# Strided attention in products of three residues, in 64 by 64 tiles of TensorE, and another order of the first batch's attention

## The chip, the cores and the metric

The kernel runs on one core of one Trainium2 chip. The metric is device time in microseconds, from the start of the program on the core to its end. Durations of single instructions come from one profiled execution.

## The reference

For 4 batches, 8 heads, 576 positions and 64 numbers a head, masked attention is computed; the first four heads look at the last 32 positions, the other four only at positions with the same remainder by 32. Two feed-forward nets follow on the 2304 rows.

```python
stride = 32
scores = scale * np.matmul(q, k.transpose(0, 1, 3, 2))
rel = pos[:, None] - pos[None, :]
mask_local = (rel >= 0) & (rel < stride)
mask_strided = (rel >= 0) & (pos[None, :] % stride == pos[:, None] % stride)
...
scores = scores - np.max(scores, axis=-1, keepdims=True)
attn = np.exp(scores)
attn = attn / (np.sum(attn, axis=-1, keepdims=True) + 1e-09)
return np.matmul(attn, v).astype(np.float32)
...
h = np.maximum(np.maximum(x @ w1, x @ w2), x @ w3)      # 512 to 768, then @ w_out to 512
g = np.maximum(h, 0.0) + alpha * np.minimum(h, 0.0)     # h = x @ w_in, 512 to 2048; then @ w_out
```

## The kernel before

The host sorts the positions of the strided heads by remainder (residue): 32 residues of 18 positions each, so that a strided head's scores are 32 blocks of 18 by 18 on the diagonal. Heads go in pairs, `cc` = 0, 1 for the local heads and 2, 3 for the strided ones; head `j` of a pair lies on 64 partitions.

`attention_tasks` handles half a pair, a unit `(b, cc, hf)`. A strided unit takes groups of six residues (108 positions, three groups) or seven (126, two groups), from the table `RG`: one product of 108 by 108 or 126 by 126 per head and group into a bank of PSUM (scores, line 353), a mask and the minimum of the negated scores on VectorE (line 361; `mask_s` for strided heads, `mask_l` and `mask_l0` for local ones), exponential and sum on ScalarE (line 368, with `accum_out`, so that each is followed by a read of the accumulator), reciprocals of the sums (lines 379, 380), normalising (on VectorE, line 397 or 394, or ScalarE, line 392), transposes on TensorE (line 408), a copy to SBUF (line 269), and the product with the values (line 437). The result is split in a high and a low part, `x`, by `part_tasks` (cast and subtraction, lines 269 and 272). Local units do the same with products of 32 by 64 (line 346), and `local_values` (line 483) does two units at once.

The nets use each number as a high and a low part: three products in place of one. A gate unit (`gate_products`, line 682) is 12 products of 288 columns with one weight tile `w`, and needs `x` of all four pairs of its half (order of the pairs: 2, 3, 0, 1). The weights arrive as 64-bit floating point numbers, and `from_double` and `split_tasks` turn them into 32-bit words and parts on ScalarE (lines 534, 543, 269) and VectorE (lines 538, 547, 550, 272). Each of the 18 gate weights of a batch's first layer is a word of this kind; they stay for the later batches.

Attention of all batches, the words and the first net of batches 0 to 2 are tasks of a planner, `Weave`: each has costs by engine, a position, needs and buffers, and the planner gives out one order, which every engine's queue then keeps. Attention of batch 0 has positions ahead of all gates, that of batches 1 to 3 lies between the gates of the batch before. SP issues all loads in one queue, in the planner's order too; a load that waits for its buffer holds those behind it. `UNREAD` puts products on a constant tile `warm_r` ahead of some tasks of TensorE (fillers, line 218); nobody reads their result. `build_constants` makes the masks and the identity on GpSimd ahead of all tasks.

Of the kernel before, what the change touches and what calls it, by code (L numbers as in the profile page):

```python
# [32 lines left out]
RG = [(0, 6), (6, 6), (12, 6), (18, 7), (25, 7)]  # L33
# [7 lines left out]
UNREAD = {(0, 3, 0): 6, ((0, 2, 0), 0): 8, ((0, 3, 0), 1): 7, ((0, 1, 0), 0): 9}  # L41
# [7 lines left out]
COST = (500, 1000)  # L49


class Weave:
# [11 lines left out]
    def __init__(self, rings):  # L64
        self.rings, self.made = dict(rings), {ring: [] for ring in rings}
        self.tasks, self.givers, self.users, self.banks, self.stores = [], {}, {}, set(), set()
        self.order = {ring: [] for ring in ("q", "v", "e", "pt", "x", "word")}
# [100 lines left out]
def attention_maxout_prelu_kernel(  # L168
# [19 lines left out]
    warm_r = const.tile([P, P], F32R, name="warm_r")  # L188
    mask_l = const.tile([QT, KW], F32, name="mask_l")
    mask_l0 = const.tile([QT, KW], F32, name="mask_l0")  # L190
    mask_s = const.tile([P, 126], F32, name="mask_s")
    alpha_sb = const.tile([P, NF2], F32, name="alpha_sb")

    def build_constants():
        g = nc.gpsimd
        nc.vector.memset(warm_r.bitcast(F32), 1.0)
        unread(bank(), WARM)
        make_identity(nc, ident)
        g.memset(mask_s, 0.0)
        ms = mask_s.rearrange("p (r a) -> p r a", a=NA)  # L200
        g.affine_select(out=ms, in_=ms, compare_op=ALU.is_ge, fill=BIG, base=0,
                        pattern=[[-NA, 7], [-1, NA]], channel_multiplier=1)
        g.affine_select(out=ms, in_=ms, compare_op=ALU.is_ge, fill=BIG, base=NA - 1,
                        pattern=[[NA, 7], [0, NA]], channel_multiplier=-1)
# [8 lines left out]
        g.memset(mask_l0[:STRIDE, :STRIDE], BIG)  # L213

# [38 lines left out]
    smp = pool(ax, "smp", 4)  # L253
    raw_p = pool(conv_x, "raw", 3, "right")
    words_p = pool(conv_x, "words", 6, "right")
    front_x = ExitStack()
    front_qk = pool(front_x, "fqk", 1, "right")
    ps = psx.enter_context(tc.tile_pool(name="ps", bufs=8, space=PSUM))
# [5 lines left out]
    weave = Weave({"bank": 8, "q": 2, "third q": 1, "v": 3, "e": 3, "pt": 4, "x": 11, "t": 4, "h": 12,  # L264
# [19 lines left out]
    def geometry(cc, hf):  # L284

        if cc < 2:
            return QT, KW, [(QT * t, QT * t, t, mask_l0 if t == 0 else mask_l)
                            for t in range(3 * hf, 3 * hf + 3)]
        gs = range(0, 3) if hf == 0 else range(3, 5)
        n = RG[gs[0]][1] * NA  # L290
        return n, n, [(RG[g][0] * NA, RG[g][0] * NA, g, mask_s) for g in gs]

    xt = {}

    def load_task(b, cc, pos):
        qk, vk = ("q", b, cc), ("v", b, cc)
# [1155 lines left out]
```

## Time and profile before

| | |
|---|---|
| time, median of 3 runs | 738.41 us (736.92 to 738.92) |
| the profiled execution's own time | 737.37 us |
| its span, first to last instruction | 735.5 us |
| granted TensorE clock | 1.00 |
| TensorE busy | 727.1 us, 99% |
| VectorE busy | 623.0 us, 85% |
| ScalarE busy | 459.1 us, 62% |
| GpSimd busy | 29.2 us, 4% |

The rows further below are read so: PE is TensorE, PEld its weight loads, DVE VectorE, ACT ScalarE, POOL GpSimd, SP the engine that issues transfers. A timeline's row gives the start, the time from the first start to the last end, the engine, the line of the kernel, the operation, output<-input, shape and count; behind it in brackets the idle time ahead of it and what ended it. Ends of products are modelled and overlap the next start, so the cost of a group is best taken from its start to the next group's start. A product of 32-bit numbers stands there twice.

### The profile page before, as it was taken

How to read it: one execution, taken by the hardware profiler on the slowest of the kernel's cores; microseconds unless marked ns; L12 is line 12 of the kernel's file. 1: busy time of each engine (PE TensorE's matmuls, PEld its weight loads, DVE VectorE, ACT ScalarE, POOL GpSimd, SP SyncE). 2: the span in 40 equal slices, each digit the busy share in tenths (PEclk: the TensorE clock that was granted, in tenths of full speed). 3: DMA queues.
4: the chain of work that ended last, by engine and by line, in shares of the span. 5: the costliest groups of instructions: out<-in, count | busy, mean ns of one | idle time of the engine just before them, and what ended most of it. 6: DMA issues, size and time to landing. Idle time of an engine off the chain costs nothing.

```text
span 735.5 us, 17464 instructions
## 1 busy us (share of the span) xinstructions
PE 727.1 (99%) x6306; PEld 706.1 (96%) x6306; DVE 623.0 (85%) x1680; ACT 459.1 (62%) x1221; POOL 29.2 (4%) x49
## 2 busy tenths in 40 slices
PE   8899999999999999999999999999999999999998
PEld 6799999999999999999999999999999999999997
DVE  5898897899898899669779988979989888888896
ACT  7997987688596676342365665625566644656561
POOL 2000000000000000055100000000000000000000
PEclk9999999999999999999999999999999999999999
DMA  8776689996998767788999799999689999867362
GB/s 294 224 262 207 220 289 343 340 326 230 361 320 298 266 231 249 244 336 317 358 326 350 252 322 327 403 381 388 238 305 308 368 401 365 296 233 253 113 206 68
DMA packets 90086, 213.63 MB, mean 290 GB/s; under 512 B 11152, under 2 KB 41360, under 8 KB 90000
## 3 DMA queue, kind: packets, MB, share of 16 engines
q1 hardware_dynamic: 90000, 212.51, 82.1%
q8 instruction: 50, 0.82, 0.4%
q14 instruction: 36, 0.29, 0.1%
HBM read 156.38 MB, written 56.10 MB: 289 GB/s over the span
## 4 chain that ended last, share of the span: by engine, by line
PE 96%; DVE 2%; ACT 1%; POOL 1%; issue 0%; POOLq 0%
PE bank L682 26%; PE ph L1289 24%; PE po L1090 15%; PE bank L704 11%; PE bank L855 5%; PE po L1096 4%; PE ph L1090 4%; PE po L1100 2%; PE bank L408 2%; PE bank L483 1%; PE bank L437 1%; PE bank L346 1%; PE bank L353 1%; ACT e L368 1%; DVE e L361 1%; PE bank L218 1%
## 5 line engine op out<-in xcount | busy, mean ns | idle before, releaser
L1289 PE MATMUL ph<-x,w 128*128 128x384 f32 x990 | 200.0, 337 | 0.0
L682 PE MATMUL bank<-x,w 128*128 128x288 f32 x1440 | 198.5, 296 | 0.0
L682 PEld LDWEIGHTS bank<-x,w 128*128 128x128 f32 x1440 | 191.9, 188 | 1.6 <-issue 0.2
L1289 PEld LDWEIGHTS ph<-x,w 128*128 128x128 f32 x990 | 166.3, 188 | 0.8
L1090 PE MATMUL po<-w,g 128*128 128x256 f32 x936 | 135.6, 281 | 0.0
L1090 PEld LDWEIGHTS po<-w,g 128*128 128x128 f32 x936 | 130.1, 189 | 0.4
L1295 DVE TENSOR_TENSOR c<-ph,c 128x384 f32<-128x384 f32 x165 | 89.5, 555 | 31.1 <-PE ph L1289 30.3
L1083 ACT CAST g<-c 128x384 fp32r<-128x384 f32 x93 | 47.2, 507 | 90.9 <-DVE c L1273 51.7
L704 PE MATMUL bank<-h,w 128*128 128x288 f32 x576 | 79.7, 297 | 0.0
L704 PEld LDWEIGHTS bank<-h,w 128*128 128x128 f32 x576 | 76.8, 188 | 0.6
L272 DVE TENSOR_TENSOR w<-word,w 128x512 fp32r<-128x512 f32 x100 | 63.2, 642 | 13.2 <-ACT w L269 12.6
L1233 ACT ACTIVATE c<-c 128x384 f32<-128x384 f32 x96 | 50.6, 528 | 33.4 <-DVE c L1295 32.3
L368 ACT ACTIVATE e<-e,nm 96x64 f32<-96x64 f32 (+2 forms) x176 | 63.5, 372 | 5.5 <-DVE nm L361 5.2
L269 ACT CAST w<-word 128x512 fp32r<-128x512 f32 x100 | 57.4, 592 | 14.7 <-DMA wh<-w 7.3
L1234 ACT ACTIVATE c<-c,nalpha 128x384 f32<-128x384 f32 x96 | 59.4, 619 | 3.1
L1238 DVE SCALAR_TENSOR_TENSOR c<-c 128x384 f32<-128x384 f32 x96 | 53.1, 553 | 5.9 <-ACT c L1234 5.9
L1084 DVE TENSOR_TENSOR g<-c,g 128x384 fp32r<-128x384 f32 x96 | 53.0, 552 | 0.9 <-ACT g L1083 0.5
L772 DVE TENSOR_TENSOR t<-bank,t 128x288 f32<-128x288 f32 x72 | 32.7, 454 | 12.8 <-PE bank L682 8.9
L1084 DVE TENSOR_TENSOR g<-k,g 128x384 fp32r<-128x384 f32 x72 | 37.1, 556 | 7.5 <-ACT g L1083 7.5
L1096 PE MATMUL po<-w,g 128*128 128x512 f32 x120 | 43.0, 398 | 0.0
L534 ACT ACTIVATE word<-raw 128x512 f32<-128x512 f32 x56 | 37.2, 683 | 8.5 <-DMA raw<-in_w 4.8
L1273 DVE TENSOR_TENSOR k<-c 128x384 f32<-128x384 f32 x72 | 37.9, 551 | 0.0
(114 smaller groups left out, 918.8 us busy)
## 6 DMA issues: line engine op xcount, KB each, us to landing
w<-wh SPq DMA_DIRECT2D x72, 512.0 KB, 5.4
raw<-in_w SPq DMA_DIRECT2D x50, 512.0 KB, 5.3
w<-wo SPq DMA_DIRECT2D x48, 512.0 KB, 5.9
w<-wp SPq DMA_DIRECT2D x36, 512.0 KB, 6.4
wh<-w SPq DMA_DIRECT2D x24, 512.0 KB, 4.4
xd<-xst SPq DMA_DIRECT2D x28, 384.0 KB, 3.2
x<-xd SPq DMA_DIRECT2D x28, 384.0 KB, 8.2
ws<-w SPq DMA_DIRECT2D x12, 512.0 KB, 4.2
```

The source lines that it names most:

```text
L269: (nc.scalar.copy if e == "ACT" else nc.vector.tensor_copy)(out_, in_)
L272: nc.vector.tensor_tensor(out=out_, in0=x, in1=y, op=ALU.subtract)
L368: nc.scalar.activation(tl[ek][:nq, j, i, :nk], tl[ek][:nq, j, i, :nk], AF.Exp, bias=tl["nm", u][:nq, j, i:i + 1], scale=-1.0, accum_out=tl ...
L682: nc.tensor.matmul(acc, words["gate", f, g][:, wi, cc * P:(cc + 1) * P], xt[b, cc, hf][:, xi, :], start=n == 0, stop=n == 3 * NCC - 1)
L704: nc.tensor.matmul(acc, words["mix", f][:, wi, dc * P:(dc + 1) * P], st["h", hf, f][:, xi, :], start=n == 0, stop=n == 3 * NF1 - 1)
L1084: return g, lambda: nc.vector.tensor_tensor(out=g[:, 1], in0=x, in1=g[:, 0].bitcast(F32), op=ALU.subtract)
L1090: nc.tensor.matmul(bank[:, NH * half:NH * (half + 1)], g[:, gi, t * P:(t + 1) * P], w[:, wi, off:off + NH], start=first and i == 0, stop=l ...
L1096: nc.tensor.matmul(bank.rearrange("p (s n) -> p s n", n=NH), g[:, 0, t * P:(t + 1) * P], w[:, :, off:off + NH], start=first, stop=last)
L1234: nc.scalar.activation(a, a, AF.Copy, scale=nalpha[:, f:f + 1])
L1238: nc.vector.scalar_tensor_tensor(out=a, in0=h, scalar=0.0, in1=a, op0=ALU.max, op1=ALU.add)
L1289: nc.tensor.matmul(bank, words["h", n, i][:, wi, off + c * P:off + (c + 1) * P], x2h[blk, k, c][:, xi, :], start=m == 0, stop=m == 5)
L1295: nc.vector.tensor_tensor(out=out_, in0=bank, in1=other, op=ALU.add)
```

## The change

Strided units are now whole pairs, `(b, cc)`, in a function of their own, `strided_tasks`. The residues are taken in threes (54 positions, 11 groups, the last of two residues; the twelfth place repeats the eleventh). A group's scores are a product of 64 by 54 per head, whose output lies on partitions 0 to 63 for even groups and 64 to 127 for odd ones, so that four products use four 64 by 64 tiles of TensorE. The exponentials lie 64 apart in one of two fixed tiles, whose gaps are zeroed once, and two groups are transposed at a time (128 by 128). The values are products of 64 by 54 in the same four tiles. `q`, `k` and `v` of strided pairs are padded on the host (608 and 768 columns in place of 576 and 640).

In the first batch the loads of all four pairs' q and k come ahead of the values', the two strided pairs and the first half of the local ones come ahead of the gates, and the second half of the local ones later, among them. Four units of this batch (`REDUCED`) have no `accum_out` in their exponentials: VectorE sums them in one reduction for each unit. GpSimd makes `mask_s` first, and the other masks and the identity in `build_more`, given out behind the first masking task. Fillers stand in other places, and the buffers of `x`, local scores and some others differ by one.

The core of the diff:

```diff
-RG = [(0, 6), (6, 6), (12, 6), (18, 7), (25, 7)]
+NR = 3
+RW = NR * NA
+NG2 = 11
+SP = S + STRIDE
-UNREAD = {(0, 3, 0): 6, ((0, 2, 0), 0): 8, ((0, 3, 0), 1): 7, ((0, 1, 0), 0): 9}
+UNREAD = {(0, 3): 2, (0, 0, 0): 2, (0, 1, 0): 3, ((0, 2), "t", 0): 4, ((0, 2), "s"): 2, ((0, 3), "s"): 3, (0, 0, 0, 0): 6}
+AFTER = {(1, 2): [("begun", 0, ("t", 0, 0, 0))]}
+REDUCED = {(0, 2), (0, 3), (0, 0, 0), (0, 1, 0)}
...
-    xp = pool(x0x, "xp", 11)
+    xp = pool(x0x, "xp", 10)
-    ep = pool(ax, "ep", 3)
+    ep = pool(ax, "ep", 2)
+    e_strided = [esp.tile([P, 2, 6, D], F32, tag=f"es{i}", name="es") for i in range(2)]
...
+    def strided_tasks(b, cc, pos, step):
+        u = (b, cc)
...
+            for g in range(12):
+                at = RW * min(g, NG2 - 1)
+                t = 2 * (g % 6 // 2) + g // 6
+                for j in range(2):
+                    rows = slice(D * j, D * (j + 1))
+                    nc.tensor.matmul(sc[j][D * (g % 2):D * (g % 2 + 1), RW * t:RW * (t + 1)],
+                                     q[rows, at:at + D], k[rows, at:at + RW], start=True, stop=True)
...
+            def masked(_, i=i):
+                for t in (2 * i, 2 * i + 1):
+                    for j in heads:
+                        nc.vector.tensor_tensor_reduce(
+                            out=tl[ek][:, j, t, :RW], in0=tl["sc", u][j][:, RW * t:RW * (t + 1)], in1=mask_s,
+                            scale=-SCALE, scalar=3.0e38, op0=ALU.add, op1=ALU.min,
+                            accum_out=tl["mx", u][:, j, t:t + 1])
+                if (u, i) == ((0, 2), 0):
+                    build_more()
...
+                        sums = {} if u in REDUCED else dict(accum_out=tl["ss", u][:, j, t:t + 1])
+                        nc.scalar.activation(e, e, AF.Exp, bias=tl["mx", u][:, j, t:t + 1], scale=-1.0, **sums)
...
+        def normalise(_):
+            e, ss, sr = tl[ek][:, :, :, :RW], tl["ss", u], tl["sr", u]
+            if u in REDUCED:
+                nc.vector.tensor_reduce(out=ss, in_=e, op=ALU.add, axis=mybir.AxisListType.X)
+            nc.vector.tensor_scalar_add(sr, ss, 1e-9)
+            nc.vector.reciprocal(sr, sr)
+            nc.vector.tensor_tensor(out=e, in0=e, in1=sr.unsqueeze(3).to_broadcast([P, 2, 6, RW]),
+                                    op=ALU.mult)
...
+                for i in range(3):
+                    nc.tensor.transpose(tr[:, P * i:P * (i + 1)],
+                                        tl[ek][:, j, 2 * i:2 * i + 2].rearrange("p t k -> p (t k)"), ident)
...
+            for g in range(6):
+                for t in range(2):
+                    n = RW if 6 * t + g < NG2 - 1 else 2 * NA
+                    if 6 * t + g < NG2:
+                        rows = slice(D * t, D * t + RW)
+                        for j in heads:
+                            nc.tensor.matmul(tl[pvs[t]][D * j:D * (j + 1), RW * g:RW * g + n], v[rows, j, g],
+                                             tl[pts[j]][rows, D * g:D * g + n], start=True, stop=True)
...
+        if b == 0:
+            when = {2: -60, 3: -56, (0, 0): -50, (1, 0): -48, ("l", 0): -43.2,
+                    (0, 1): -4, (1, 1): -2, ("l", 1): 2.8}
+            loads = {("q", 2): -80, ("q", 3): -79, ("q", 0): -78, ("q", 1): -76, ("v", 2): -54, ("v", 3): -52,
+                     ("v", 0, 0): -44, ("v", 1, 0): -44 + 0.5, ("v", 0, 1): -6, ("v", 1, 1): -6 + 0.5}
+            attention(b, when, loads, 2.4)
+            continue
```

What stands where on the engines. First TensorE at the end of the first batch's attention, before; L346 are local scores, L353 strided scores, L408 transposes, L483 local values, L218 fillers, and L682 gate products.

```order
L346 MATMUL bank<-k,q 32x64 x18
L218 MATMUL bank<-warm_r 128x512 x9
L408 MATMUL bank<-ident,e 128x96 x3
L353 MATMUL bank<-k,q 108x108 x6
L483 MATMUL bank<-pt,v 64x32 x36
L408 MATMUL bank<-ident,e 128x96 x3
L353 MATMUL bank<-k,q 126x126 x4
L682 MATMUL bank<-x,w 128x288 x12
L408 MATMUL bank<-ident,e 128x96 x3
L682 MATMUL bank<-x,w 128x288 x12
L483 MATMUL bank<-pt,v 64x32 x36
L682 MATMUL bank<-x,w 128x288 x216
```

The same place after, from the transposes of the first half on; here L397 are local transposes, L352 local scores, L426 local values, L228 fillers, L740 gate products, and L465 strided scores of batch 1.

```order
L397 MATMUL bank<-ident,e 128x96 x3
L352 MATMUL bank<-k,q 32x64 x18
L397 MATMUL bank<-ident,e 128x96 x3
L352 MATMUL bank<-k,q 32x64 x18
L426 MATMUL bank<-pt,v 64x32 x36
L228 MATMUL bank<-warm_r 128x512 x6
L740 MATMUL bank<-x,w 128x288 x36
L397 MATMUL bank<-ident,e 128x96 x6
L740 MATMUL bank<-x,w 128x288 x12
L426 MATMUL bank<-pt,v 64x32 x36
L465 MATMUL bank<-k,q 64x54 x24
L740 MATMUL bank<-x,w 128x288 x192
```

Three gate units now stand ahead of the second half's transposes, and four ahead of its values, where two stood behind nearly all of the batch's attention.

ScalarE at its beginning, before: L368 are exponentials with their sums, L269 copies of transposed scores (`pt`) and casts of `x`, L534 the first step of a word.

```order
L368 ACTIVATE e,sm<-e,nm 108x108 x6
L368 ACTIVATE e,sm<-e,nm 126x126 x4
L368 ACTIVATE e,sm<-e,nm 108x108 x4
L269 COPY pt<-bank 108x324 x2
L368 ACTIVATE e,sm<-e,nm 108x108 x2
L269 COPY pt<-bank 126x252 x2
L368 ACTIVATE e,sm<-e,nm 126x126 x2
L269 CAST x<-bank 128x9x18 x2
L368 ACTIVATE e,sm<-e,nm 126x126 x2
L269 CAST x<-bank 128x9x14 x2
L368 ACTIVATE e,sm<-e,nm 96x64 x6
L534 ACTIVATE word<-raw 128x512 x2
```

The same after: L487 are strided exponentials and L368 local ones, both without sums here, L283 copies and casts, L590 and L599 steps of words.

```order
L487 ACTIVATE es<-es,mx 128x54 x24
L368 ACTIVATE e<-e,nm 96x64 x8
L283 COPY pt<-bank 128x384 x2
L368 ACTIVATE e<-e,nm 96x64 x4
L590 ACTIVATE word<-raw 128x512
L283 CAST x<-bank 128x9x18
L283 CAST x<-bank 128x9x14
L283 CAST x<-bank 128x9x18
L283 CAST x<-bank 128x9x14
L599 ACTIVATE raw<-raw 128x512
L283 COPY pt<-bank 128x384 x2
L590 ACTIVATE word<-raw 128x512 x2
```

The exponentials of both strided pairs now come in a row, with eight of the local ones, ahead of the first copies.

TensorE among the gates of batch 0, where batch 1's first strided pair is worked on, before (names as above; L437 are strided values):

```order
L408 MATMUL bank<-ident,e 108x108 x6
L408 MATMUL bank<-ident,e 126x126 x4
L682 MATMUL bank<-x,w 128x288 x36
L437 MATMUL bank<-pt,v 64x108 x6
L353 MATMUL bank<-k,q 108x108 x6
L353 MATMUL bank<-k,q 126x126 x4
L682 MATMUL bank<-x,w 128x288 x24
L437 MATMUL bank<-pt,v 64x126 x4
```

The same after; L511 are strided transposes, L535 strided values.

```order
L511 MATMUL bank<-ident,es 128x128 x6
L740 MATMUL bank<-x,w 128x288 x36
L535 MATMUL bank<-pt,v 64x54 x18
L535 MATMUL bank<-pt,v 64x36 x2
L535 MATMUL bank<-pt,v 64x54 x2
L465 MATMUL bank<-k,q 64x54 x24
```

A pair's values now stand in one place instead of two, in 22 small products instead of ten.

## Rows read from the trace of the kernel before

**Rows 1.** The page: TensorE's busy time, and its granted clock in 40 slices

```profile
PE 727.1 (99%) x6306; PEld 706.1 (96%) x6306; DVE 623.0 (85%) x1680; ACT 459.1 (62%) x1221; POOL 29.2 (4%) x49
...
PEclk9999999999999999999999999999999999999999
```

**Rows 2.** TensorE's timeline from 36 us on

```profile
36.09 28.83 PE L682 MATMUL bank<-x,w 128*128 128x288 f32 x216
64.77 1.15 PE L408 MATMUL bank<-ident,e 108*108 108x108 f32 x10
65.67 5.04 PE L682 MATMUL bank<-x,w 128*128 128x288 f32 x36
70.64 0.78 PE L437 MATMUL bank<-pt,v 108*64 108x108 f32 x12
71.35 1.28 PE L353 MATMUL bank<-k,q 64*108 64x108 f32 x20
72.55 3.44 PE L682 MATMUL bank<-x,w 128*128 128x288 f32 x24
75.93 0.65 PE L437 MATMUL bank<-pt,v 126*64 126x126 f32 x8
76.51 5.03 PE L682 MATMUL bank<-x,w 128*128 128x288 f32 x36
81.47 0.62 PE L346 MATMUL bank<-k,q 64*32 64x64 f32 x36
...
117.62 1.25 PE L483 MATMUL bank<-pt,v 64*64 64x32 f32 x72
```

**Rows 3.** TensorE's timeline, 0 to 36 us

```profile
4.77 1.94 PE L353 MATMUL bank<-k,q 64*108 64x108 f32 x20
...
16.92 0.49 PE L408 MATMUL bank<-ident,e 108*108 108x108 f32 x3 [1.69 <-DVE e L397]
...
25.14 2.34 PE L218 MATMUL bank<-warm_r 128*128 128x512 f32 x9
...
30.64 1.85 PE L682 MATMUL bank<-x,w 128*128 128x288 f32 x12
```

**Rows 4.** VectorE's timeline, 0 to 40 us

```profile
6.34 0.27 DVE L361 CUSTOM_DVE_ANT_0 e<-bank,mask_s 108x108 f32<-108x108 f32 x1 [5.33 <-POOL mask_l L213]
...
14.76 0.22 DVE L361 CUSTOM_DVE_ANT_0 e<-bank,mask_l 96x64 f32<-96x64 f32 x1 [0.68 <-PE bank L346]
14.90 0.08 DVE L361 DVE_READ_ACCUMULATOR2_ANT nm<- 96x1 f32 x1
...
23.53 0.55 DVE L394 TENSOR_TENSOR e<-e,rc 96x384 f32<-96x384 f32 x1
```

**Rows 5.** Busy time by stretch: PE, PEld, DVE, ACT, POOL, clock

```profile
36.10:50.00 13.90, 13.90 (x110) 13.90 (x106) 12.92 (x30) 13.62 (x44) 0.00 (x0) 1.00 0.80 276
```

**Rows 6.** ScalarE's timeline, 0 to 46 us

```profile
6.66 0.39 ACT L368 ACTIVATE e<-e,nm 108x108 f32<-108x108 f32 x1 [4.63 <-DVE nm L361]
...
11.92 0.74 ACT L269 COPY pt<-bank 108x324 f32<-108x324 f32 x2
...
16.03 0.38 ACT L368 ACTIVATE e<-e,nm 96x64 f32<-96x64 f32 x1
16.28 0.22 ACT L368 ACTIVATION_READ_ACCUMULATOR e<-e,nm 96x1 f32 x1
16.37 0.37 ACT L368 ACTIVATE e<-e,nm 96x64 f32<-96x64 f32 x1
...
44.13 1.01 ACT L392 ACTIVATE e<-e,rc 108x108 f32<-108x108 f32 x3
44.98 0.73 ACT L534 ACTIVATE word<-raw 128x512 f32<-128x512 f32 x1
```

**Rows 7.** Transfers issued in the first 40 us: median us to landing

```profile
raw<-in_w SPq DMA_DIRECT2D x8, 512.0 KB, 5.3
...
k<-in_kTs SPq DMA_DIRECT2D x4, 288.0 KB, 4.3
```

More of the change, by code (lines that the diff above doesn't have):

```diff
@@ L66, in __init__ @@
         self.tasks, self.givers, self.users, self.banks, self.stores = [], {}, {}, set(), set()
-        self.order = {ring: [] for ring in ("q", "v", "e", "pt", "x", "word")}
+        self.order = {ring: [] for ring in ("q", "v", "e", "es", "pt", "x", "word")}
     def add(self, engines, emit, pos, needs=(), gives=(), makes=(), uses=(), mode=None, slack=0):
@@ L197, in build_constants, with build_more @@
         unread(bank(), WARM)
-        make_identity(nc, ident)
[L199 to L204, printed above, removed]
+        g.memset(mask_s, 0.0)
+        for q in range(0, P, D):
+            m = mask_s[q:q + D].rearrange("p (r a) -> p r a", a=NA)
+            g.affine_select(out=m, in_=m, compare_op=ALU.is_ge, fill=BIG, base=0,
+                            pattern=[[-NA, NR], [-1, NA]], channel_multiplier=1)
+            g.affine_select(out=m, in_=m, compare_op=ALU.is_ge, fill=BIG, base=NA - 1,
+                            pattern=[[NA, NR], [0, NA]], channel_multiplier=-1)
+    def build_more():
+        g = nc.gpsimd
+        make_identity(nc, ident)
         for m in (mask_l0, mask_l):
@@ L469, in local_values @@
+    def local_values(b, hf, pos):
         vks = [("v", b, cc, hf) for cc in range(2)]
-        pts = [("pt", (b, cc, hf), 0) for cc in range(2)]
+        pts = [("pt", (b, cc, hf)) for cc in range(2)]
         pvs = [("pv", b, hf, j) for j in range(2)]
@@ L992, in attention_maxout_prelu_kernel, with attention @@
     build_constants()
-    for b in range(B):
-        first, last = (-32, -8) if b == 0 else ((b - 1) * NUNITS + (16 if b == 1 else 3), b * NUNITS - 3)
-        step = (last - first) / (len(ATT_UNITS) + 2)
-        for i, (cc, hf) in enumerate(ATT_UNITS):
-            if i in (0, 2, 4, 5):
-                load_task(b, cc, first + step * i - 8)
-            if cc < 2:
-                values_task(("v", b, cc, hf), vl[b, cc, hf], first + step * i - 7)
-            attention_tasks(b, cc, hf, first + step * i, step)
+    def attention(b, when, loads, step):
+        for cc in (2, 3):
+            load_task(b, cc, loads["q", cc])
+            values_task(("v", b, cc), vs[b, cc - 2], loads["v", cc])
+            strided_tasks(b, cc, when[cc], step)
+        for hf in range(2):
+            for cc in range(2):
+                if hf == 0:
+                    load_task(b, cc, loads["q", cc])
+                values_task(("v", b, cc, hf), vl[b, cc, hf], loads["v", cc, hf])
+                local_tasks(b, cc, hf, when[cc, hf], step)
+            local_values(b, hf, when["l", hf])
@@ new lines, in attention_maxout_prelu_kernel @@
+    for b in range(B):
+        if b == 0:
[5 more added lines that the diff above has]
+            continue
+        first, last = (b - 1) * NUNITS + (16 if b == 1 else 3), b * NUNITS - 3
+        step = (last - first) / 10
+        order = [2, None, 3, None, (0, 0), (1, 0), (0, 1), (1, 1)]
+        when = {u: first + step * i for i, u in enumerate(order) if u}
+        loads = {("q", cc): when[cc if cc > 1 else (cc, 0)] - 8 for cc in range(4)}
+        loads |= {("v", u) if u in (2, 3) else ("v", *u): when[u] - 7 for u in when}
+        when |= {("l", 0): when[1, 0] + 2 * step, ("l", 1): when[1, 1] + 2 * step}
+        attention(b, when, loads, step)
```

313 lines of the change are left out of this document (157 added, 156 removed).

## The prediction

> **What bounds the kernel now.** I read the page's busy shares first: TensorE is busy 99% of the span, and its granted clock is full in all 40 slices [rows 1]. So the first question was whether that is throughput or a chain of waits that looks like work. TensorE's own timeline answers it for the two parts. From 36.1 us on it shows no idle time before any group; there the time is the sum of what TensorE executes [rows 2]. Before 36.1 us it is different: TensorE runs fillers on `warm_r` whose results nobody reads, stands idle for 1.69 us on VectorE's normalised scores, and does the first gate products only at 30.64 us [rows 3]. So the front is bounded by the attention of the first batch on the other engines. Their timelines show which: VectorE begins masking at 6.34 us, released by the last write of `mask_l`, although it masks with `mask_s` [rows 4], and ScalarE starts 0.3 us later, at 6.66 [rows 6]. Even from 36.1 to 50 us, when TensorE no longer waits, ScalarE is busy 13.62 of 13.90 us and VectorE 12.92 [rows 5]. I therefore cost the change in two pieces: TensorE's work after the front, and the chain on ScalarE and VectorE in it.
>
> **Strided units in batches 1 to 3 (TensorE).** Today one strided pair of heads costs, from start to start: transposes 64.77 to 65.67 = 0.90 us, values 0.71 + 0.58, scores 71.35 to 72.55 = 1.20; 3.39 us together [rows 2]. No row shows a 64 by 54 product. The rows follow a sum: (stationary columns + 2 x streamed columns) / 2.4 GHz / tiles at work. It gives 58 ns for the values of 108 columns (108 by 64, two tiles side by side), measured 0.71/12 = 59; 66 for 126 columns, measured 72. For 64 by 54 with four tiles it gives (64 + 108)/2.4/4 = 18 ns. Bounds: the two forms that already run in four or more tiles, 36 in 0.62 and 72 in 1.25 us busy, show 17 ns each whatever they stream, so not much less than 16; if only two tiles worked at a time, 36 ns. I take 18, since the form with 64 stationary columns in four tiles is the nearest row. The trace counts each of these products twice: the new scores are 48 instructions (0.86 us), the values 44 (0.79). Transposes become six of 128 by 128; today's ten of 108 and 126 columns take 0.90 us, 0.8 ns a column, so 6 x 0.105 = 0.63. New unit 2.28 us, saving 1.11. Six units: 6.7 us, less 0.34 for the scores of batch 1's first unit, which both kernels do in the front: 6.3.
>
> Each place where attention interrupts the gates costs something besides: 36 gate products take 4.97 us after one and 24 take 3.38, where the undisturbed rate of 216 in 28.68 us gives 4.78 and 3.19, so 0.19 each [rows 2]. The order holds 36 such places before and 32 after: 0.8 us saved. Sum for batches 1 to 3: **-7.1 us**.
>
> VectorE and ScalarE don't take this back: 12 masks of 54 columns (650 columns) replace ten of 108 and 126 (1150), two pairs of reciprocal steps become one, and normalising leaves ScalarE (three of 108 columns occupied it from 44.13 to 44.98) [rows 6]. In batches 1 to 3 each has less to do.
>
> **The front.** I compare at one point: all attention of batch 0 done, four gate units done, the scores of batch 1's first strided unit done. Before: 36.1 us with two units done, so 36.1 + 2 x 1.6 = 39.3. After, step by step:
> - `mask_s` no longer waits for the other masks (VectorE waited 5.33 us, until 6.34 [rows 4]). TensorE begins its scores at 4.77 us behind the fillers, as now [rows 3]; 0.86 plus 0.2 for the first ones (20 took 1.94 us there and 1.28 later [rows 2, 3]) gives 5.85, first mask 5.95: only 0.4 us earlier. The second unit's q and k move up in SP's queue, ahead of the values; a k takes 4.3 us to land [rows 7], and it is there near 6.7, before VectorE needs it.
> - ScalarE: 24 exponentials of 54 columns and 12 of 64 without the accumulator's read. With it one of 64 columns takes 0.25 + 0.09 us [rows 6]. Without it is not in the trace. Upper bound: only the read goes, so 0.245 for 64 columns and 0.235 for 54; the scaling copies, which also take an operand of one value per partition and have no read, show 0.85/3 = 0.28 for 108 columns, and (0.28 - 0.245)/44 is 0.8 ns a column. Lower bound: a plain copy, 0.37 for 324 columns [rows 6], less 270 columns at that rate, 0.15. I take the upper one, by the nearest row. ScalarE then ends the 24 at 6.25 + 5.64 = 11.9, the 8 local ones queued ahead at 13.9, and only then the two copies of transposed scores (0.37 each): 14.6.
> - VectorE has 24 masks, six local ones (0.145 each), then a reduction over 648 numbers (no row; a multiply of 384 takes 0.55 [rows 4], so between 0.5 and 1.0, I take 0.75), two short operations and the product of 648 numbers: 12.2. So ScalarE, not VectorE, paces here.
> - Values of the first unit 14.75 to 15.55; words (a step of 512 columns takes 0.73 with its tail [rows 6], 0.55 to the next) and casts on ScalarE, copies of the second unit 18.45; its values end at 19.4; casts, local copies, a word: 22.3. Local values 1.2, then six fillers (nine take 2.34 us [rows 3]): first gate product at **25.0** instead of 30.64. VectorE has x and the first word ready by 24.6, behind the second half's twelve masks, which stand ahead of them in its queue.
> - Three gate units to 29.9. Behind them stand the transposes of the second half, whose exponentials (12 with the read, 0.33 each) share ScalarE with words and casts until 29.5; normalised 30.4. The fourth gate unit waits for its word: 31.3. Its raw data are issued behind values loads that wait for buffers; 5.3 us to land [rows 7] still lets ScalarE have it in time. Then 1.6, local values 1.2, scores 1.0: **35.1** against 39.3, **-4.2 us**. With the lower price of the exponentials it would be 33.9.
>
> After that point the gates need one new word for most units, and ScalarE and VectorE, which make them, are both near full [rows 5]; gates that start earlier could outrun them. What covers this: ScalarE loses some 5 us of exponentials in the front. That is part of the 4.2.
>
> **Smaller things.** One x buffer and one local score buffer fewer: in the new order batch 2's first gate unit follows its local values with only six transposes between. Casting and subtracting x (288 columns, twice in turn; by a copy of 324 in 0.37 [rows 6] and a product of 384 in 0.55 [rows 4], 0.3 and 0.4 each) take about as long as those and half a unit: 0 to 1.3 us, I take 0.5. The larger transfers of q and values (5 to 20% more) move under TensorE's work; were the first ones not hidden, 5% more of a k that takes 4.3 us to land [rows 7] would be 0.2 us.
>
> Sum: -7.1 - 4.2 + 0.5 = -10.8 us. The profiled execution took 737.4 (span 735.5 and 1.9 around it), 1.0 below the median of three: 726.6 in its terms, 727.6 in those of the median. I say **727.5**.
>
> **Rivals.**
> 1. The front's gain is given back: words come late, and TensorE waits inside the first 20 gate units. For it speak the two full engines; against it ScalarE's shorter front. Then only batches 1 to 3 gain: 738.4 - 7.1 + 0.5 = 732.
> 2. The smaller product has a fixed cost that doesn't shrink. 17 ns for both 32 and 64 streamed columns hints at one. Suppose a 54-column product costs half of what one of 108 to 126 does now (1.20/20 = 60 ns): 30 ns, a unit 3.4 us, no saving but that of the places: some 734. Against it, the same 17 ns. The Trainium skill, TensorEngine Tiling (Array Packing), section Performance Considerations, says that a matmul has about 60 cycles of overhead and that a tiling factor should not be taken from a dimension that is already small. An estimate by that figure is 25 ns an instruction, a unit of 2.9 us, and some 731. The trace's 17 ns rows speak against as much as that.
> 3. Slower: the four tiles don't overlap, because two of them write one bank of PSUM. 72 ns an instruction, a unit 7.2 us, 23 us more in batches 1 to 3, and the front's gain gone: some 760. It decides from 38 ns an instruction on (fewer than two tiles at a time). The local values' 72 products write in the same pattern at 17 ns.
>
> **Numbers.** Forecast 0.67, rival 1 0.18, rival 2 0.08, rival 3 0.03, 0.04 for what I don't see. The range takes the tiles' and exponentials' lower bounds and no late x below (-0.6, -1.2, -0.5, and up to 3 for a front that overlaps better than my chain), and rivals 1 and 2 above: 722 to 733. A difference under 0.3%, 2.2 us, can't be told from none here: faster 0.92, within 0.04, slower 0.04.
>
> **What will show it.** The 48 scores of a strided unit in batches 1 to 3 take 0.8 to 0.9 us and its 44 values 0.8; if 1.2 or more, rival 2 or 3. First mask near 6.0 us, first gate product near 25, the fifth unit near 35; no idle time on TensorE afterwards. If gates start at 25 but idle time stands before gate products until 60 us, on words, it is rival 1. If an exponential without the read takes 0.15 us, the front is shorter by about one microsecond. It is wrong if the gates stretch after 60 us shows waits that today's doesn't.

## The result, and the profile after

The changed kernel takes **732.2 us** (median of 4 runs, 731.31 to 733.20) against 738.66 in the same job: ratio 0.9916 (95% interval 0.9894 to 0.9939), 6.4 us faster. Forecast were 727.5, so 4.7 us of gain are missing. The profiled execution took 731.31, its span is 729.5 (735.5 before).

TensorE's busy time and granted clock on the page, which answer to [rows 1]:

```profile
PE 716.4 (98%) x6682; PEld 698.0 (96%) x6682; DVE 615.0 (84%) x1680; ACT 446.0 (61%) x1180; POOL 30.3 (4%) x53
...
PEclk9999999999999999999999999999999999999999
```

TensorE's timeline to 61 us, against [rows 3], and from 123 us, against [rows 2]; L465 are the new scores, L511 the transposes, L535 the values, L740 the gates:

```profile
4.76 1.39 PE L465 MATMUL bank<-k,q 64*64 64x54 f32 x48
...
14.56 1.27 PE L535 MATMUL bank<-pt,v 54*64 54x54 f32 x44 [0.46 <-ACT pt L283]
...
24.59 4.95 PE L740 MATMUL bank<-x,w 128*128 128x288 f32 x36
...
34.88 25.65 PE L740 MATMUL bank<-x,w 128*128 128x288 f32 x192
60.37 0.82 PE L511 MATMUL bank<-ident,es 128*128 128x128 f32 x6
60.94 5.00 PE L740 MATMUL bank<-x,w 128*128 128x288 f32 x36
...
123.11 0.92 PE L465 MATMUL bank<-k,q 64*64 64x54 f32 x48
123.96 9.82 PE L740 MATMUL bank<-x,w 128*128 128x288 f32 x72
...
138.62 0.91 PE L535 MATMUL bank<-pt,v 54*64 54x54 f32 x44
139.45 6.62 PE L740 MATMUL bank<-x,w 128*128 128x288 f32 x48
```

By starts, a strided unit now costs 0.85 + 0.57 + 0.83 = 2.25 us (3.39 before), and the point that the forecast put at 35.1 us is at 34.88. So both pieces of the change came about as forecast. The rest is found by walking on to the end. The last batch's net, `last_net` (line 844), stands outside the planner. Before its 12 gate units VectorE makes 8 sums (line 864) and 8 differences (line 870) of parts of `x`, whose splits are factors T1 to T4 of the last gates' pair products (line 913). At the same place SP begins to load rows of x for the second net, for which GpSimd makes sums and splits. The changed kernel's TensorE from there on:

```profile
291.03 14.44 PE L740 MATMUL bank<-x,w 128*128 128x288 f32 x108
308.69 6.61 PE L740 MATMUL bank<-x,w 128*128 128x288 f32 x36 [3.22 <-DVE t L751]
315.14 3.33 PE L913 MATMUL bank<-x,w 128*128 128x288 f32 x24
318.87 30.95 PE L913 MATMUL bank<-x,w 128*128 128x288 f32 x228 [0.40 <-ACT x L233]
349.65 19.26 PE L762 MATMUL bank<-h,w 128*128 128x288 f32 x144
369.67 2.37 PE L1369 MATMUL ph<-x,w 128*128 128x384 f32 x12 [0.76 <-ACT xo L969]
372.59 2.36 PE L1369 MATMUL po<-x,w 128*128 128x384 f32 x12 [0.55 <-ACT xo L969]
374.79 2.24 PE L1369 MATMUL ph<-x,w 128*128 128x384 f32 x12
```

And the kernel before:

```profile
304.21 19.20 PE L682 MATMUL bank<-x,w 128*128 128x288 f32 x144
323.25 33.78 PE L855 MATMUL bank<-x,w 128*128 128x288 f32 x252
356.86 19.24 PE L704 MATMUL bank<-h,w 128*128 128x288 f32 x144
375.94 2.24 PE L1289 MATMUL ph<-x,w 128*128 128x384 f32 x12
...
380.10 2.24 PE L1289 MATMUL ph<-x,w 128*128 128x384 f32 x12
```

TensorE reaches the last net 13.2 us earlier (291.03 for 304.21), and the third group of the second net's products only 5.3 us earlier (374.79 for 380.10). I call the stretch between them the **hand-over**: 75.9 us before, without a wait; 83.8 after. There 7.9 us were given back. VectorE's timeline, first in the changed kernel, then in the one before, shows the first reason:

```profile
297.74 0.43 DVE L286 TENSOR_TENSOR w<-word,w 128x256 fp32r<-128x256 f32 x1 [0.66 <-ACT w L283]
301.16 1.56 DVE L864 TENSOR_TENSOR xs<-x 128x288 f32<-128x288 f32 x4 [3.00 <-DMA wp<-w]
...
308.18 0.45 DVE L751 TENSOR_TENSOR t<-bank,t 128x288 f32<-128x288 f32 x1
```

```profile
305.15 0.42 DVE L272 TENSOR_TENSOR w<-word,w 128x256 fp32r<-128x256 f32 x1 [3.25 <-ACT w L269]
305.49 1.56 DVE L806 TENSOR_TENSOR xs<-x 128x288 f32<-128x288 f32 x4
```

L286 (L272 before) splits the last words of the planner. Before, VectorE began the last split 0.9 us after TensorE came to the last net; now it begins it 6.7 us after. Then the first sum waits 3.00 us for a store of words, whose third buffer lies where the rows `xs` are put. So the sums begin 10.1 us after TensorE's arrival, before 1.3. The maxima that read the first gate units out of TensorE's banks (L751), and so free them, stand behind the sums. TensorE does 9 units, finds no free bank and stops for 3.22 us; the next 36 products take 0.179 us each instead of 0.132, with a granted clock of 0.89 from 300 to 315 us (a mean over the stretch, between 2.4 GHz, which is 1, and 1.2).

### The profile page after: what moved, and what is told of

It reads as the page before. It is cut to its first block, busy times and chain, and to the rows that moved or that the text cites. A ratio compares the mean times of both kernels' runs of the same rounds, so it can differ in the third digit from the quotient of the medians.

```text
span 729.5 us, 18174 instructions
## 1 busy us (share of the span) xinstructions
PE 716.4 (98%) x6682; PEld 698.0 (96%) x6682; DVE 615.0 (84%) x1680; ACT 446.0 (61%) x1180; POOL 30.3 (4%) x53
## 4 chain that ended last, share of the span: by engine, by line
PE 92%; DVE 3%; ACT 3%; DMA 2%; issue 1%; SPq 0%; DVEq 0%; ACTq 0%
PE ph L1369 24%; PE bank L740 24%; PE po L1170 15%; PE bank L762 10%; PE bank L913 4%; PE po L1176 4%; PE ph L1170 4%; PE po L1180 2%; PE bank L426 1%; DMA wp<-w 1%; PE bank L352 1%; PE bank L465 1%; ACT es L487 1%; PE bank L535 1%; DMA raw<-in_w 1%
## 5 line engine op out<-in xcount | busy, mean ns | idle before, releaser
L740 PE MATMUL bank<-x,w 128*128 128x288 f32 x1440 | 199.4, 298 | 3.4 <-DVE t L751 3.2
L740 PEld LDWEIGHTS bank<-x,w 128*128 128x128 f32 x1440 | 193.5, 190 | 5.2 <-DVE t L751 3.5
L286 DVE TENSOR_TENSOR w<-word,w 128x512 fp32r<-128x512 f32 x100 | 63.6, 643 | 13.2 <-ACT w L283 12.5
L283 ACT CAST w<-word 128x512 fp32r<-128x512 f32 x100 | 57.6, 587 | 24.7 <-DMA wp<-w 8.5
L590 ACT ACTIVATE word<-raw 128x512 f32<-128x512 f32 x56 | 36.8, 675 | 5.7 <-DMA raw<-in_w 4.6
L1163 ACT CAST g<-k 128x384 fp32r<-128x384 f32 x72 | 33.1, 514 | 7.1 <-PE po L1176 3.3
```

The source lines that it names most:

```text
L283: (nc.scalar.copy if e == "ACT" else nc.vector.tensor_copy)(out_, in_)
L286: nc.vector.tensor_tensor(out=out_, in0=x, in1=y, op=ALU.subtract)
L740: nc.tensor.matmul(acc, words["gate", f, g][:, wi, cc * P:(cc + 1) * P], xt[b, cc, hf][:, xi, :], start=n == 0, stop=n == 3 * NCC - 1)
L1163: cast(g[:, 0], x)
```

## The experiments

In the table, "words" is the time from the last net's first gate product to the start of VectorE's last word split, and "GpSimd" the start of its first sum for the second net; both and the hand-over come from the profiled execution, the ratio is to the kernel before in the same job.

| kernel | us | ratio, 95% interval | words | GpSimd | hand-over |
|---|---|---|---|---|---|
| before | 738.66 | | 0.9 | 317.5 | 75.9 |
| changed | 732.2 | 0.9916 (0.9894, 0.9939) | 6.7 | 311.4 | 83.8 |
| sums later | 730.23 | 0.9883 (0.9863, 0.9904) | 6.7 | 313.4 | 81.4 |
| rows elsewhere | 729.36 | 0.9871 (0.9848, 0.9895) | 6.7 | 310.2 | 80.6 |
| both | 729.44 | 0.9875 (0.9853, 0.9898) | 6.7 | 309.7 | 80.2 |
| two units twice | 736.23 | 0.9957 (0.9941, 0.9973) | 6.8 | 311.7 | 88.3 |
| before, with both | 742.06 | 1.0048 (1.0036, 1.0060) | 0.9 | 321.7 | 78.2 |
| both, words closer | 729.38 | 0.9871 (0.9857, 0.9886) | 6.8 | 310.9 | 81.0 |
| old front order | 739.35 | 1.0010 (0.9996, 1.0025) | 7.4 | 319.0 | 83.5 |
| accumulator | 736.30 | 0.9970 (0.9956, 0.9983) | 7.6 | 316.6 | 83.5 |
| both, 8 sums on GpSimd | 728.14 | 0.9854 (0.9834, 0.9875) | 7.6 | 311.2 | 80.2 |
| both, 16 on GpSimd | 730.16 | 0.9893 (0.9874, 0.9912) | 10.2 | 312.7 | 81.1 |
| both, loads first | 732.25 | 0.9913 (0.9894, 0.9933) | 6.7 | 306.1 | 83.9 |
| both, 16 and loads first | 730.14 | 0.9889 (0.9868, 0.9910) | 10.4 | 311.7 | 82.4 |

**Sums later.**

```diff
+        def sums():
...
         for n, (hf, f, g) in enumerate(units(GATES_LAST)):
             gate_unit(b, hf, f, g, st)
-            if n < 6:
-                make(n)
+            if n == 2:
+                sums()
+            for m in {2: range(2), **{i: (i - 1,) for i in range(2+1, 7)}}.get(n, ()):
+                make(m)
```

> The changed kernel, with VectorE's 24 sums of the last net (lines 864 and 870) and the first two splits emitted after the third gate unit instead of ahead of the first; nothing is left out. Theory (the gain is given back at the hand-over because the sums, which wait for word stores, stand ahead of the greatest of the first units on VectorE, so that TensorE finds 8 full accumulators): the idle 3.22 us before the 36 gate products at 308.7 us goes, and with it most of the 1.7 us by which these products ran slow (0.179 us each for 0.132); 732.2 - 4.9 + up to 1 for later loads = 728 us (726.5 to 729.5), granted clock from 300 to 350 us at 1.00. Rival (the end hangs on the chain word stores, sums, splits, loads of the second hand-over, and TensorE's idle time is only where that slack shows): 731.5 us or more, the same idle time found again on TensorE before 380 us.

(What moves are 16 operations, 8 sums and 8 differences, not 24.)

**Rows elsewhere** (and **both**, which is these two edits).

```diff
-    xsp = pool(ctx, "xsp", 2, "right")
     tsp = pool(ctx, "tsp", 3, "right")
+    xsp = pool(ctx, "xsp", 2, "right")
```

> The changed kernel, with the three temporaries tsp placed in memory where the rows xs stood, so that the rows no longer lie on the third buffer of the word stores; the order of all instructions is as it was, nothing is left out. Theory (the first sum's 3.00 us wait is for the store out of that buffer): the sums start at about 298.2 us instead of 301.2, TensorE's idle 3.22 us shrinks to 0.2 and the slow products mostly go: 727.5 us (726.5 to 729.5). Rival A (the sums wait for something else that ends at the same time, ScalarE's or VectorE's last word splits): sums start at 300.5 or later, 731 to 732 us. Rival B (the end hangs on the words themselves, which reach the stores no earlier): sums start earlier, end unchanged, 731.5 us or more.

> Both edits together: sums after the third gate unit, rows off the store's buffer. Theory: either edit alone takes the whole idle time, so the two are worth no more than one, 727.5 us (726 to 729), and TensorE runs from 291 us to its wait at about 365 us without an idle time over 0.5 us. Rival (the chain from the sums to the loads of the second hand-over ends last): only the earlier sums count, and the two together give 1 to 3 us more than the better of them.

Each takes TensorE's 3.22 us away, as the theory had it, but only 2.0, 2.8 and 2.8 us of the time, not the 4 to 5 forecast (no run of the three is as slow as a run of the changed kernel, though the intervals of the ratios overlap a little). A wait comes up in its place: 2.56 us with the sums later, 2.36 with the rows elsewhere, and with both:

```profile
290.59 19.20 PE L740 MATMUL bank<-x,w 128*128 128x288 f32 x144
309.63 3.35 PE L917 MATMUL bank<-x,w 128*128 128x288 f32 x24
315.08 0.40 PE L917 MATMUL bank<-x,w 128*128 128x288 f32 x1 [2.10 <-ACT x L233]
315.84 31.91 PE L917 MATMUL bank<-x,w 128*128 128x288 f32 x227 [0.36 <-DVE x L236]
...
366.66 2.25 PE L1373 MATMUL ph<-x,w 128*128 128x384 f32 x12
```

The 25th pair product (L917 is the line 913 of the changed kernel) waits for factor T4, which is split behind everything that VectorE has piled up. In the changed kernel this wait was 0.40 us, since TensorE came to it late. So my theory had the place right and the price wrong: the wait was one of two, at the same backlog.

**Two units twice.**

```diff
+            if n < 2:
+                gate_products(b, hf, f, g)
             gate_unit(b, hf, f, g, st)
```

> The changed kernel, with the 12 products of each of the last net's first two gate units done twice, the first time into an accumulator that nobody reads: 24 more products of 0.132 us, 3.2 us more work for TensorE just ahead of its wait; nothing is left out. Theory (TensorE has slack there, and the sums set when it goes on): the idle time falls from 3.22 to about 0, the products after it run at 0.132 us since the clock no longer falls, and the time stays at 731 to 732.5 us. Rival (TensorE's work is the bound there too): 735 to 735.5 us.

The time was the rival's, 736.2, but not by the rival's way:

```profile
291.33 22.76 PE L740 MATMUL bank<-x,w 128*128 128x288 f32 x168
...
319.25 30.93 PE L915 MATMUL bank<-x,w 128*128 128x288 f32 x228 [1.98 <-ACT x L233]
350.02 19.33 PE L762 MATMUL bank<-h,w 128*128 128x288 f32 x144
370.53 1.31 PE L1371 MATMUL ph<-x,w 128*128 128x384 f32 x6 [1.18 <-ACT xo L971]
373.79 2.29 PE L1371 MATMUL ph<-x,w 128*128 128x384 f32 x6 [1.95 <-ACT xo L971]
375.88 3.93 PE L1371 MATMUL po<-x,w 128*128 128x384 f32 x12
```

The 24 extra products (3.2 us) are absorbed: lines 913 and 762 go on at 319.25 and 350.02, 0.4 us later than in the changed kernel. TensorE does have slack at the last net. Then 4.5 us are lost at the start of the second net: waits for ScalarE's `xo` copies, one of which stood 2.14 us on a store, and 12 products in 3.93 us for 2.24, with a granted clock of 0.77 from 365 to 380 us. Why 0.4 us become 4.5 there I can't say.

**Before, with both.** The kernel before with the two edits above.

> The kernel before, with both edits of the hand-over to the last net (sums after the third gate unit, rows off the store's buffer) and nothing of the change; nothing is left out. Theory (before, TensorE reached the last net only 1.3 us ahead of the sums' start, with no idle time after it, so nothing was to be had there; the loss came with the change): 738.4 us, 737 to 739.7, and 75.9 us from the last net's first gate product to the third group of products of the second hand-over, as before. Rival (the sums and the rows' place bound the kernel before as well, and the edits are a gain of their own): 736 us or less.

Neither: it is 3.4 us slower. There the sums are ready to go 1.3 us after TensorE's arrival (at 305.11 us in this run), so putting them behind three units starts them at 311.40 us instead of 305.49:

```profile
311.40 1.55 DVE L809 TENSOR_TENSOR xs<-x 128x288 f32<-128x288 f32 x4
```

```profile
327.90 30.40 PE L859 MATMUL bank<-x,w 128*128 128x288 f32 x227 [0.27 <-DVE x L226]
```

With the two together nothing was to be had in the kernel before, and the order that was right for it is wrong after the change. The run also shows how much there was to spare: the sums begin 6.3 us after TensorE's arrival, and at the pair products TensorE waits 0.27 us for VectorE. So some 5 us more of delay cost next to nothing at that place (most of the 2.3 us that this hand-over is longer stand further on, 1.20 of them in a wait for `xo`).

**Both, words closer.**

```diff
-    pace = 2.6
+    pace = 2.4
```

> The kernel with both hand-over edits, and the word tasks of the second layers placed 2.4 units apart in the plan instead of 2.6, so that they are issued earlier on ScalarE, VectorE and the queue; nothing is left out. Theory (the words were paced to the old, slower TensorE: VectorE ends them 7 us after TensorE has come to the last net, 1 us before the change, and its backlog of words, sums and greatest sets the T4 factor for which TensorE waits 2.1 us): the last word split ends by 295 us instead of 297.7, TensorE's wait at its 25th product of the last net's pairs goes, 726 us (724.5 to 727.8). Rival (the words are bound by transfers, whose share is 0.91 to 0.97 in four stretches of 30 us): they end no earlier, or TensorE waits in batches 1 to 3 instead; 729 us or more.

The rival's time: the last word split comes 6.8 us after TensorE, as without the edit. At this spacing at least, the place of the words in the plan isn't what makes them late. In the changed kernel ScalarE's last word casts wait for the buffers of earlier stores:

```profile
293.16 0.62 ACT L283 CAST w<-word 128x512 fp32r<-128x512 f32 x1 [0.86 <-DMA ws<-w]
295.73 0.62 ACT L283 CAST w<-word 128x512 fp32r<-128x512 f32 x1 [1.95 <-DMA wp<-w]
297.30 0.41 ACT L283 CAST w<-word 128x256 fp32r<-128x256 f32 x1 [0.95 <-DMA wo<-w]
```

Whether a fourth such buffer would bring the words earlier isn't shown.

**Old front order.** The branch `if b == 0` and the new places of the first words go; the placing of the kernel before takes their place.

```diff
-        if b == 0: ...
-        first, last = (b - 1) * NUNITS + (16 if b == 1 else 3), b * NUNITS - 3
+        first, last = (-32, -8) if b == 0 else ((b - 1) * NUNITS + (16 if b == 1 else 3), b * NUNITS - 3)
```

> The changed kernel with its new products, but the first batch's attention and the first gate words placed as in the kernel before (halves not in turn, loads not first); fillers and VectorE's sums of four units stay. Theory (the front's order is worth the 4.2 us that were forecast, less the hand-over's loss): the first 192 gate products in one run start at 38.5 to 39.5 us instead of 34.9; the end 2.5 to 4.5 us later, 734.7 to 736.7 us. Rival (the front's gain is given back wholly at the hand-over, where the words set the time): the same later start, but 732 to 733 us.

Slower than either: +7.1 us in the median (its runs spread from 736.4 to 741.9), +5.1 in the profiled span, in which the last net begins 5.3 us later. The hand-over is 83.5 us, near the changed kernel's 83.8, so nothing of the front's gain is given back there. What the order is worth is less clear. At the point by which the front was forecast this run is 4.0 us later: 180 gate products start at 36.41 us, and one gate unit of them and the scores that stand behind them (1.6 and 0.85 us) make 38.9, for 34.88. That is near the 4.2 us that I gave it. Another 1.3 us come between there and the last net, and the profiled run is the fastest of twelve, so the rest of the 7.1 us isn't in the trace. The fillers stand for the new order, too: TensorE waits 3.04 us at 20 us, and its granted clock is 0.66 from 20 to 30 us.

**Accumulator.**

```diff
-REDUCED = {(0, 2), (0, 3), (0, 0, 0), (0, 1, 0)}
+REDUCED = set()
```

> The changed kernel, with ScalarE's accumulator in place of VectorE's sums for all units of the first batch, as the later batches have it: each exponential is followed by an accumulator read (0.33 us for the two where they stand in later batches, against 0.231 alone in the front). Theory (ScalarE paces the front): 24 exponentials by 0.10 = 2.4 us more ahead of the first transposes' copies; first gate product at 26.5 to 27 us instead of 24.6, the time 733 to 734.5 us. Rival (VectorE paces the front, and its 6 sums of 0.82 us each are on the path): first gate product at 24 us or earlier, 732 us or less.

ScalarE's 24 exponentials with their reads take 7.76 us (6.74 to 14.50); without, in the changed kernel, 5.55. TensorE in this kernel:

```profile
23.07 0.57 PE L397 MATMUL bank<-ident,e 96*128 96x96 f32 x3 [2.99 <-ACT word L590]
...
29.48 3.64 PE L740 MATMUL bank<-x,w 128*128 128x288 f32 x24
...
38.75 25.69 PE L740 MATMUL bank<-x,w 128*128 128x288 f32 x192
```

The first gate product comes at 29.48 us, not 26.5 to 27, and not by the theory's way. The planner chooses the engine of the copies by its costs, and with dearer exponentials it gave the first unit's copies to VectorE; the first values start at 15.06 us for 14.56. The delay comes at the local units, whose 12 exponentials have the read as well (the theory counted only 24 of the 36): the transposes above stand 2.6 us later than in the changed kernel (23.07 for 20.46). Behind the idle 2.99 us the granted clock is 0.54 from 23 to 26 us and 0.50 from 26 to 29, which is the level of 1.2 GHz, and that adds 2.3 us up to the first gate product. The run of 192 starts 3.9 us later than in the changed kernel (38.75 for 34.88), and by the medians the end is 4.1 us later. VectorE, which loses four sums here (two of 0.82 us and two of 0.54, not six of 0.82), doesn't pace the front. That ScalarE does fits the run, but what a microsecond of it is worth can't be read from it, since copies and clock changed with the accumulator. What the front loses is lost at the end.

**8 sums, then all 16, on GpSimd**, with both edits.

```diff
-                        nc.vector.tensor_tensor(out=rows[i][r][:, h, :HALF], ...)
+                        nc.gpsimd.tensor_tensor(out=rows[i][r][:, h, :HALF], ...)
...
-                    nc.vector.tensor_tensor(out=out_, in0=x, in1=y, op=ALU.subtract)
+                    nc.gpsimd.tensor_tensor(out=out_, in0=x, in1=y, op=ALU.subtract)
```

> The kernel with both hand-over edits, and the last net's 8 sums of line 864 on GpSimd instead of VectorE; nothing is left out. In the run with both edits VectorE is busy from its last word split at 297.3 us to 316 us, and TensorE waits 2.10, 0.40 and 0.36 us for the T4 and T1 factors' splits, which stand at that backlog's end. Theory (the rest of what the hand-over gives back is VectorE's backlog): 8 sums of 0.39 us leave it, 3.1 us, TensorE's wait of 2.9 us falls to under 0.5, the 227 products after it run at 0.133 us instead of 0.140 (1.5 us): 725.5 us (724.5 to 727). Rival (TensorE waits there for the words or for ScalarE, or what is saved is lost at the second hand-over as with two units done twice): 728.5 us or more.

> As the one before, with the 8 differences of line 870 on GpSimd as well. GpSimd takes 1.0 to 1.1 us for such a sum of 128 by 384, so about 0.85 for 128 by 288, 13.6 us for the 16; it has nothing else to do from 36 us on, and their inputs are there at about 283 us, so they can end near 298 us, about when VectorE ends the words. Theory: VectorE's backlog falls by 6.7 us, no wait of TensorE from 291 to 366 us, 725 us (724 to 726.5), about the run before less what is left of its wait. Rival A (GpSimd's sums come later or slow VectorE's words by sharing its memory port): the wait moves to the T1 and T2 factors, 728 us or more. Rival B (nothing is left to win once 8 sums are moved): equal to the run before.

With 8 moved, TensorE's waits for these splits fall to 1.08 + 0.52 us, and the time of 728.1 is the best of all, below the changed kernel's by intervals that don't meet, but above the forecast 725.5 and its range. With 16 moved, the time is rival A's, the place of the waits is not:

```profile
291.47 19.20 PE L740 MATMUL bank<-x,w 128*128 128x288 f32 x144
310.51 23.31 PE L917 MATMUL bank<-x,w 128*128 128x288 f32 x174
334.43 11.00 PE L917 MATMUL bank<-x,w 128*128 128x288 f32 x78 [0.61 <-ACT t L935]
...
367.11 2.36 PE L1373 MATMUL ph<-x,w 128*128 128x384 f32 x12 [0.75 <-ACT xo L973]
370.36 2.38 PE L1373 MATMUL po<-x,w 128*128 128x384 f32 x12 [0.89 <-ACT xo L973]
```

TensorE runs from 291.47 to 334 us without a wait, so the first wait is VectorE's backlog: shown. The words are later still here, 10.2 us behind TensorE, so it isn't their lateness by itself that TensorE waits for, but what stands behind them on VectorE. But what is won comes back as five waits behind it (three stand here, the others are 0.79 and 0.24 us, on the parts of `h`); the hand-over stays at 81.1 us. GpSimd's sums also held up VectorE (last section).

**Loads first**, without and with the 16 sums on GpSimd.

```diff
+    early_load(1, 0, xsu, "xst")
     for n, _ in enumerate(last_net(B - 1)):
...
-            if n == X_SPLIT + 21 * half - 8:
+            if half and n == X_SPLIT + 10:
                 early_load(1, half, xsp, "xs")
...
-            early_split(*ready[n], (xst, xsu)[n // 2 % 2])
+            early_split(*ready[n], (xst, xsu)[n // 2 % 2] if ready[n][1] else xsp if ready[n][2] in (1, 3) else xst)
```

> The kernel with both hand-over edits, and the loads of the rows of x for the second layers (line 986, GpSimd's input) taken ahead: the first four at the head of the last net into a buffer of their own, the next four 3 units earlier; the sums stay on VectorE, nothing is left out. In all runs so far but the one with units done twice, the third group of products of the second hand-over came 60 to 63.4 us after GpSimd's first sum, whatever TensorE did. Theory (two limits in a row: VectorE's backlog at the first hand-over, and GpSimd's chain from these loads to the second): the chain starts 2 to 4 us earlier, but with both edits TensorE waited only at the first hand-over (2.9 us) and not at the second, so this alone changes little: 728 to 730 us. Rival (that chain alone sets the end): the end follows GpSimd's first sum, 725.5 to 727 us.

> The same loads ahead, and all 16 sums of the last net on GpSimd. Theory (two limits in a row): each edit alone moved TensorE's wait to the other place, and the two together take both; from the last net's first gate product to the third group of the second hand-over 76.5 to 78 us, near the 75.9 of the kernel before, where TensorE never waited: 731.3 - 83.8 + 77.2 = 724.7 us, with the spread of the front 723.5 to 726.5. Rival (GpSimd, with 38 operations of about 1 us in a row, is itself the limit, or a third wait comes up): no better than the better of the two alone, 728 us or more.

Both failed by waits that the edits brought themselves: 732.25 us is outside either forecast of the first, 730.14 is the rival's for the second. In the first, GpSimd starts 5.3 us earlier than in the changed kernel, then waits 5.52 us for ScalarE's first cast and 5.72 for one that itself waited 6.22 us for a store out of a buffer that the splits now share, and the end is no earlier. That also ends the rule that the third group comes 60 to 63.4 us after GpSimd's first sum; here it comes 69 us after. In the second, TensorE waits 3.25 us for loads of the pair factors. They are issued at 307.56 us, behind the loads taken ahead and behind the stores of words; in the first, behind the same loads, at 301.94, and there TensorE has no such wait. Between the two stand the 16 sums on GpSimd, with which the word stores are issued up to 304.8 us instead of 299.2. The two limits in a row are therefore neither shown nor refuted.

## Why the prediction was right in kind and 4.7 us too far

**Batches 1 to 3** (-7.1, and +0.5 for the near tie). From the end of the front (39.3 worked out before, 34.88 after) to the last net it took 264.9 us and now takes 256.1: -8.8. Scores were priced at 0.86 us, values 0.79, transposes 0.63; measured 0.85, 0.83 and 0.57. Four tiles do work side by side: 0.85/48 is 18 ns, as the sum for four tiles gave. (The sum isn't a rule, though: for the old scores, 20 instructions in 1.20 us, it gives 1.44.) That settles rival 2. The Trainium skill, TensorEngine Tiling (Array Packing), section Performance Considerations, gives about 60 cycles of overhead a matmul. I had charged it to one instruction after another, 25 ns each by estimate, and the trace's 18 ns are less. Whether each tile pays it isn't shown, since with four at work a tile has 71 ns for each product of its own. Rival 3 fell by the same rows. The tie at batch 2 didn't come. Of the 2.2 us more than the forecast's 6.6, 0.5 are that tie and 1.5 the strided units: the six old ones took 3.55 us on average, more than the one I had priced at 3.39, and the new ones 2.18. The rest lies in the local parts.

**The front** (-4.2). First mask at 6.33 us for 5.95: with `mask_s` made first VectorE waits 5.34 us for TensorE's scores, where it had waited 5.33 for `mask_l`, so the masks' order gave nothing by itself. Exponentials 0.231 us for 0.235, first gate product 24.59 for 25.0, the common point 34.88 for 35.1. The accumulator's run speaks for ScalarE pacing it.

**Rival 1** names the measured time, 732, by a way that wasn't taken, and the range holds that time only by the room left for rivals 1 and 2. TensorE has no wait from 34.88 us to the last net, and the two runs with a slower front keep the hand-over at 83.5 us: the front's gain reaches the last net and isn't eaten there.

**The step that failed** is in the first paragraph: "there the time is the sum of what TensorE executes", from 36.1 us to the end, and with it "no idle time on TensorE afterwards". By its own last sign, waits in the gates stretch that the kernel before doesn't have, the prediction failed here: the 3.22 us ahead of the gate products at 308.69 us are one. It read the absence of waits in the kernel before as a property of the kernel. It was one of the balance: at the last net VectorE's sums began 1.3 us behind TensorE and could have come some 5 us later before TensorE waited for them; now they begin 10.1 us behind. Sum: -4.4 (front) - 8.8 (batches 1 to 3) + 7.9 (hand-over) - 0.7 (behind it) = -6.0, the difference of the spans.

Shown of the 7.9: TensorE's first wait is for VectorE, for sums behind a store's buffer and ahead of the maxima, then for VectorE's backlog; the two edits give back 3.5 us of the hand-over, 2.8 of the time. Only argued: that the words are late because batches 1 to 3 now take 8.8 us less while words, their stores and three buffers are the same. For it speak the last word split, which comes 265.9 us after the end of the front before and 262.9 now, 3.0 us less where TensorE takes 8.8 less; the lag of 6.7 to 7.6 us in all kernels with the new products but the two with 16 sums on GpSimd, whatever the front or the plan's spacing, and ScalarE's waits for stores. Open: the 4.3 to 5.5 us that the hand-over keeps over the 75.9 in the better versions, when one wait is removed and another appears.

## What to carry to other kernels

An engine that is busy 99% bounds a kernel only as far as the next one is behind it. Before adding up what a bound engine saves, look in each stage at how late its suppliers end, and how late they may: here VectorE's sums began 1.3 us behind TensorE's arrival and then 10.1, and at that hand-over 7.9 of 13.2 us went. Code that is issued by hand behind a plan (sums ahead of the releases of banks, a buffer laid on another's place) is ordered for one arrival, and is to be looked at again when the arrival moves. A right time isn't a right reason: rival 1 hit 732 without its mechanism.

## What the hardware showed that I hadn't expected

GpSimd's sums slow VectorE at the same time. VectorE's groups from 283 to 302 us, in the changed kernel and with all 16 sums on GpSimd (count, busy us, mean ns):

```profile
L286 DVE TENSOR_TENSOR w<-word,w 128x512 fp32r<-128x512 f32 (+1 forms) x9 | 5.6, 630 | 5.2 <-ACT w L283 5.2
L682 DVE TENSOR_TENSOR word<-word 128x256 f32<-128x256 f32 x4 | 1.6, 421 | 0.1
```

```profile
L286 DVE TENSOR_TENSOR w<-word,w 128x512 fp32r<-128x512 f32 (+1 forms) x9 | 8.9, 1019 | 2.1 <-ACT w L283 2.1
L682 DVE TENSOR_TENSOR word<-word 128x256 f32<-128x256 f32 x4 | 3.8, 967 | 0.1
```

Operations with two inputs in SBUF take 1.6 to 2.3 times as long, and the last word split comes 10.2 us after TensorE instead of 6.7. With 8 sums, over by 291.7 us, the four of L682 come behind them and take 418 ns. The Trainium skill, SBUF — State Buffer, section SBUF: two separate sides, says that VectorE and GpSimd share one pair of ports under an exclusive lock, which VectorE's instructions with two SBUF inputs need too when GpSimd's reads SBUF. The rows agree in kind, with 967 ns for 421.

A wait of TensorE can cost more than its length. Behind the 3.22 us the next 36 products were 1.7 us slower in sum (granted clock 0.70 from 310 to 315 us), behind the waits of 1.18 and 1.95 us in the run with two units twice 12 were 1.7 us slower, with both edits the granted clock was 0.66 from 315 to 320 us behind 2.10 us, and with the accumulator 0.50 to 0.54 for 6 us behind 2.99 us. But not every wait did: behind 2.36 us with the rows elsewhere, and 1.98 us with two units twice, the clock stayed at 1.00, and the next 228 products took 0.135 us each, as in the changed kernel.
